# Token columns of the feed-forward products: 448 and 448 taken as 512 and 384, with one more float32 product

## The chip, the cores and the metric

The kernel runs on one core of a Trainium2 chip. The metric is device microseconds of one execution. The core has TensorE for matrix products (its results go to PSUM, which has eight banks of 512 float32 columns for each of 128 partitions), ScalarE and VectorE for elementwise work, GpSimd for elementwise work on SBUF, and SyncE, which issues the transfers. In the rows below they are PE (PEld for its weight loads), ACT, DVE, POOL and SP.

## The reference

Causal attention over 2 batches, 12 heads, 448 tokens and 64 columns a head, then two feed-forward blocks on the 896 tokens of both batches:

```python
attn = softmax(mask(q @ k.T / 8)) @ v       # per head; then as x: 896 x 768
a, b = x @ w1, x @ w2                       # 768 x 1024 each
x = ((a * b) @ w3) @ w_out                  # 1024 x 1024, 1024 x 768
h = x @ w_in                                # 768 x 2048
out = (maximum(h, 0) ** 2) @ w_out2         # 2048 x 768
```

All inputs are float32. The two weights w3 and w_out of the first block are multiplied with each other by the kernel, so that (a * b) meets one matrix W = w3 w_out of 1024 x 768.

## The kernel before

A float32 product is made of three products of the type float32r (L448): each operand is split into a high part and a rest, and high x high, high x rest and rest x high are added up in one PSUM bank. Plain float32 products are used where one product of full width stands alone (the attention, and `pause`).

The first part (L363 to L439) has attention, in an order written out by hand for TensorE, VectorE and ScalarE. In between it splits weights and multiplies w3 by w_out in slices of 384 columns (`w_half`, the tiles w of L69 with hl_wout). Attention leaves `xT`: the tokens as columns, both batches side by side, 2 x 448 = 896, in a high part and a rest.

What follows (L442 on) is the part that the change touches. Weights stand still on TensorE in tiles of 128 x 128 and tokens stream past them as columns, in two pieces of 448, one for each batch and each in a PSUM bank of its own. `products` (L446) gives the three float32r products of one weight tile for both pieces; the pieces take turns within each. The stages, in the names of the rows:

- **w** (`w12`, L475): 8 column tiles m of w1 and of w2, each summed over KD = 6 weight tiles. For the first EARLY = 2 tiles m, batch 0 is computed by itself ahead and batch 1 later; for the other six both pieces together. `ab` (L486) multiplies the two results (ScalarE copy, VectorE product) and splits them into `abT` (ScalarE, GpSimd).
- **h** (L510): 6 column tiles of W, each summed over KF = 8 tiles; `h_parts` splits into `hT` with ScalarE and VectorE. The last two tiles run together.
- **g** (L523) and **o** (L538), twice, for the two halves of 2048: g is 8 column tiles of w_in over 6 weight tiles, then relu and square on ScalarE (L533, L534) and the split into `gT` (ScalarE L119, GpSimd L120). o multiplies by the second w_out; here tokens stand still, 7 tiles of 128, and the 768 columns of w_out stream in two pieces of HN = 384.

`banks` (L455) gives out PSUM tiles in turn from two pools that hold the eight banks. `pause` (L462) is a plain float32 product of 64 columns of a weight tile with itself, into the bank that the next product overwrites, so that its result is of no use. It stands ahead of the first w product (after the 384-wide products of W) and ahead of the second g stage (after the 384-wide products of o).

The order in this part is that of a scheduler, which here keeps the order in which the code is written for TensorE. In the trace all products have line L69 (the helper `mm`), so tiles tell them apart: w, h, g, o. Split weights come through a ring of 8 buffers; loading, decoding and splitting them runs on SP, ScalarE and VectorE beside the products.

Of the kernel before, what the change touches and what calls it, by code (L numbers as in the profile page):

```python
# [8 lines left out]
F32 = mybir.dt.float32  # L9
F32R = mybir.dt.float32r  # L10
U32 = mybir.dt.uint32
AF = mybir.ActivationFunctionType
ALU = mybir.AluOpType
# [4 lines left out]
def attention_moe_moe2(ctx: ExitStack, tc: tile.TileContext, qk, v, w1, w2, w3, w_out, w_in2, w_out2, out):  # L18
# [13 lines left out]
    nc = tc.nc  # L32
    NP_ALL, P, S2 = qk.shape
    S = S2 // 2
    _, CP, _ = v.shape
    NT, DM = out.shape
    D = P // 2
    NCH = S // CP
    B = NT // S
    NPAIR = NP_ALL // B  # L40
    KD = DM // P
    KF = w1.shape[0]
    KF2 = w_in2.shape[0]
    HN = DM // 2
# [14 lines left out]
    EARLY = 2  # L59
# [8 lines left out]
    def mm(o, l, r, start, stop):  # L68
        return nc.tensor.matmul(o, l, r, start=start, stop=stop)  # L69
# [48 lines left out]
    def two_parts(hi, lo, x, engine=None):  # L118
        nc.scalar.copy(hi, x)  # L119
        (engine or nc.vector).tensor_tensor(lo, x, hi.bitcast(F32), op=ALU.subtract)  # L120
# [49 lines left out]
    def used(key):  # L170

        n = in_ring[key] + RING
        if n < len(ring):
            make(ring[n])
# [4 lines left out]
    with (  # L179
# [144 lines left out]
        parts = [key for key in order if not (key[0] == "w3" and key[1] < PLAIN)]  # L324
# [117 lines left out]
    tmp = ctx.enter_context(tc.tile_pool(name="tmp", bufs=4, reuse_waits="tile"))  # L442
    big2 = ctx.enter_context(tc.tile_pool(name="big2", bufs=1, reuse_waits="tile"))
    ps = ctx.enter_context(tc.tile_pool(name="ps", bufs=6, space=PSUM, reuse_waits="tile"))

    def products(o, wt, col, x, kk, start, stop, bs=(0, 1)):  # L446

        for s, t in ((0, 0), (0, 1), (1, 0)):  # L448
            for b in bs:
                mm(o[b], wt[:, s, col], x(kk)[:, t, b * S:(b + 1) * S],  # L450
                   start and (s, t) == (0, 0), stop and (s, t) == (1, 0))

    turn = [0]

    def banks(names, width=S):  # L455

        n = turn[0]
        turn[0] += len(names)
        where = [(ps_w, "w") if (n + i) % 8 < 2 else (ps, "mm") for i in range(len(names))]
        return [pool.tile([P, width], F32, tag=tag, name=m) for m, (pool, tag) in zip(names, where)]  # L460

    def pause(o, wt):  # L462

        x = wt[:, 0, :P].bitcast(F32)
        mm(o[:, :PAUSE], x, x[:, :PAUSE], True, True)

    def two_banks(name):
        return banks([f"{name}_{b}" for b in range(2)])

    def g_tiles(name):  # L470
        return [big2.tile([P, 2, NT], F32R, tag=f"G{m}", name=f"{name}{m}") for m in range(KF)]

    g_t = g_tiles("abT")

    def w12(m, bs):  # L475
        o = {}
        for nm in ("w1", "w2"):
            o[nm] = dict(zip(bs, banks([f"{nm}_{m}_{b}" for b in bs])))
            if nm == "w1" and m == 0 and 0 in bs:
                pause(o[nm][0], hls[nm, m])  # L480
            for kk in range(KD):
                products(o[nm], hls[nm, m], slice(kk * P, (kk + 1) * P), lambda c: xT[:, :, c], kk,
                         kk == 0, kk == KD - 1, bs)
        return o

    def ab(m, bs, o):  # L486
        for b in bs:
            a = tmp.tile([P, S], F32, tag="t", name=f"a{m}_{b}")
            nc.scalar.copy(a, o["w1"][b])
            nc.vector.tensor_tensor(a, o["w2"][b], a, op=ALU.mult)  # L490
            two_parts(*(g_t[m][:, s, b * S:(b + 1) * S] for s in range(2)), a, nc.gpsimd)

    os = [w12(m, (0,)) for m in range(EARLY)]
    for m in range(KF):
        if m < EARLY:
            ab(m, (0,), os[m])
        bs = (1,) if m < EARLY else (0, 1)
        ab(m, bs, w12(m, bs))
        used(("w1", m))
        used(("w2", m))  # L500

    hT = big.tile([P, 2, KD, NT], F32R, tag="X", name="hT")

    def h_parts(j, o):
        for b in range(2):
            hi, lo = (hT[:, s, j, b * S:(b + 1) * S] for s in range(2))
            nc.scalar.copy(hi, o[b])
            nc.vector.tensor_tensor(lo, o[b], hi.bitcast(F32), op=ALU.subtract)

    for js in [(j,) for j in range(KD - 2)] + [(KD - 2, KD - 1)]:  # L510
        o = [two_banks(f"h{j}") for j in js]
        for i in range(KF):
            for j, oj in zip(js, o):
                products(oj, hls["W", i], slice(j * P, (j + 1) * P), lambda c: g_t[c], i, i == 0, i == KF - 1)
            if len(js) > 1:
                used(("W", i))
        for j, oj in zip(js, o):
            h_parts(j, oj)

    acc = big.tile([P, NTT, DM], F32, tag="W", name="acc")  # L520
    for g in range(KF2 // KF):
        g_t = g_tiles(f"gT{g}_")
        for mi in range(KF):  # L523
            m = g * KF + mi
            o = two_banks(f"g{m}")
            if mi == 0 and g > 0:
                pause(o[0], hls["win2", m])
            for kk in range(KD):
                products(o, hls["win2", m], slice(kk * P, (kk + 1) * P), lambda c: hT[:, :, c], kk,
                         kk == 0, kk == KD - 1)  # L530
            for b in range(2):
                r = tmp.tile([P, S], F32, tag="t", name=f"r{m}_{b}")
                nc.scalar.activation(r, o[b], AF.Relu)  # L533
                nc.scalar.activation(r, r, AF.Square)  # L534
                two_parts(*(g_t[mi][:, s, b * S:(b + 1) * S] for s in range(2)), r, nc.gpsimd)
            used(("win2", m))
        ends = [(NTT - 2, NTT - 1)] if g == 0 else [(NTT - 2,), (NTT - 1,)]
        for ts in [(t,) for t in range(NTT - 2)] + ends:  # L538
            os = [banks([f"o{g}_{t}_{n}" for n in range(2)], HN) for t in ts]
            final = g > 0 and ts[0] == NTT - 1  # L540
            for ns in ((0,), (1,)) if final else ((0, 1),):
                for fi in range(KF):
                    w = hls["wout2", g * KF + fi]
                    for t, o in zip(ts, os):
                        for s, r in ((0, 0), (0, 1), (1, 0)):
                            for n in ns:
                                mm(o[n], g_t[fi][:, s, t * P:(t + 1) * P], w[:, r, n * HN:(n + 1) * HN],
                                   fi == 0 and (s, r) == (0, 0), fi == KF - 1 and (s, r) == (1, 0))
                    if len(ts) > 1:
                        used(("wout2", g * KF + fi))  # L550
            for t, o in zip(ts, os):
                for n in range(2):
                    a = acc[:, t, n * HN:(n + 1) * HN]
                    if g == 0:
                        if n == 0:
                            nc.scalar.copy(a, o[n])
                        else:
                            nc.vector.tensor_copy(a, o[n])
                    else:
                        nc.vector.tensor_tensor(a, o[n], a, op=ALU.add)  # L560
                        if final:
                            nc.sync.dma_start(out=out[t * P:(t + 1) * P, n * HN:(n + 1) * HN], in_=a)
                if g > 0 and not final:
                    nc.sync.dma_start(out=out[t * P:(t + 1) * P, :], in_=acc[:, t, :])
# [48 lines left out]
```

## Time and profile before

| | us |
|---|---|
| median of 3 runs | 577.47 (577.46 to 577.71) |
| the profiled execution | 577.6 |
| its span, first to last instruction | 575.4 |
| TensorE busy (products) | 563.9, 98% of the span |
| TensorE weight loads | 506.5, 88% |
| VectorE | 281.3, 49% |
| ScalarE | 268.2, 47% |
| GpSimd | 159.1, 28% |

The span is cut into attention (to about 161 us), w (to 280), h (to 339), g (to 397), o (to 455), g again (to 514) and o again (to 572). A busy TensorE is not a TensorE at its best, since a product's record covers its way through the array and overlaps the next one's. What tells the cost of a product in an unbroken stream is the length of the stream divided by its count, and that is how the rows are used below. The record's own length matters only where records of one kind are compared.

### The profile page before, as it was taken

What the parts mean: (1) busy time and instruction counts of PE and PEld (TensorE: products, weight loads), DVE (VectorE), ACT (ScalarE), POOL (GpSimd) and SP (SyncE); (2) the same over time, 40 slices, a digit from 0 to 9 for tenths busy, and PEclk for the clock granted to TensorE, in tenths of its full rate; (3) what the DMA queues carried; (4) which work ended last, traced back from release to release, by engine and by line L of the source; (5) the groups of instructions that cost most, each with busy time, mean ns of one, the idle gap of its engine ahead of it and who ended that gap; (6) DMA issues with size and microseconds to landing.
All of it is one profiled execution on the core that took longest, in us unless ns stands there. A gap on an engine that the chain in (4) does not pass through costs nothing.

```text
span 575.4 us, 8129 instructions
## 1 busy us (share of the span) xinstructions
PE 563.9 (98%) x3144; PEld 506.5 (88%) x3144; DVE 281.3 (49%) x567; ACT 268.2 (47%) x574; POOL 159.1 (28%) x140
## 2 busy tenths in 40 slices
PE   7899999999999999999999999999999999999997
PEld 5557777778989999999999999999999999999997
DVE  5987887767687544222210484555102854421011
ACT  5778777757865533222210456666002666640000
POOL 3367677776200312111100003333000023330000
PEclk9999999999999999999999999999999999999999
DMA  8854554233266633000000274333100763000111
GB/s 318 288 194 140 177 159 159 84 124 120 88 225 245 204 120 107 9 1 1 1 1 0 67 271 156 109 111 110 56 1 4 270 219 110 1 1 29 56 55 56
DMA packets 14823, 63.96 MB, mean 111 GB/s; under 512 B 1665, under 2 KB 1921, under 8 KB 14785
## 3 DMA queue, kind: packets, MB, share of 16 engines
q1 hardware_dynamic: 14784, 63.45, 32.2%
q8 instruction: 25, 0.41, 0.3%
q14 instruction: 14, 0.11, 0.1%
HBM read 60.69 MB, written 2.75 MB: 110 GB/s over the span
## 4 chain that ended last, share of the span: by engine, by line
PE 86%; DVE 6%; ACT 5%; issue 1%; DMA 1%; DVEq 0%; ACTq 0%
PE w L69 28%; PE g L69 20%; PE o L69 20%; PE h L69 10%; PE s L69 3%; PE x L69 2%; PE pp L273 2%; ACT p L245 2%; ACT pt L277 2%; DVE p L238 1%; DVE xw L108 1%; DMA qk<-in_qk 1%; ACT hl_wout L90 1%; DVE raw_wout L103 0%; DVE x_wout L108 0%
## 5 line engine op out<-in xcount | busy, mean ns | idle before, releaser
L69 PE MATMUL g<-hT,hl_win 128*128 128x448 f32 x576 | 117.2, 365 | 0.0
L69 PE MATMUL w<-xT,hl_w 128*128 128x448 f32 x576 | 117.0, 365 | 0.0
L69 PE MATMUL o<-hl_wout,gT 128*128 128x384 f32 x672 | 116.9, 334 | 0.0
L69 PEld LDWEIGHTS o<-hl_wout,gT 128*128 128x128 f32 x672 | 116.6, 188 | 0.1
L69 PEld LDWEIGHTS g<-hT,hl_win 128*128 128x128 f32 x576 | 108.1, 188 | 8.5
L69 PEld LDWEIGHTS w<-xT,hl_w 128*128 128x128 f32 x576 | 108.1, 188 | 8.5
L255 POOL TENSOR_SCALAR p<-p,st 112x448 f32<-112x448 f32 (+1 forms) x84 | 96.5, 1166 | 51.9 <-DVE st L252 23.3
L120 POOL TENSOR_TENSOR gT<-r,gT 128x448 fp32r<-128x448 f32 x32 | 39.1, 1245 | 195.8 <-ACT gT L119 128.7
L69 PE MATMUL w<-hl_wout,w 128*128 128x384 f32 x336 | 64.4, 342 | 0.5 <-DVE w L106 0.3
L245 ACT ACTIVATE p<-p,st 112x448 f32<-112x448 f32 (+1 forms) x96 | 49.7, 530 | 27.1 <-DVE st L238 27.0
L69 PEld LDWEIGHTS w<-hl_wout,w 128*128 128x128 f32 x336 | 57.4, 188 | 3.9 <-issue 0.9
L69 PE MATMUL h<-abT,hl_W 128*128 128x448 f32 x288 | 58.5, 365 | 0.0
L69 PEld LDWEIGHTS h<-abT,hl_W 128*128 128x128 f32 x288 | 54.1, 188 | 4.3
L120 POOL TENSOR_TENSOR abT<-a,abT 128x448 fp32r<-128x448 f32 x16 | 21.8, 1377 | 111.8 <-ACT abT L119 111.8
L238 DVE CUSTOM_DVE_ANT_0 p<-s,mask 112x448 f32<-112x448 f32 (+1 forms) x96 | 36.5, 441 | 7.0 <-PE s L69 7.0
L106 DVE TENSOR_TENSOR hl_wout<-x_wout,hl_wout 128x768 fp32r<-128x768 f32 x20 | 19.1, 957 | 37.9 <-ACT hl_wout L90 37.9
L533 ACT ACTIVATE r<-g 128x448 f32<-128x448 f32 x32 | 15.8, 542 | 40.8 <-PE g L69 40.8
L69 PE MATMUL s<-qk 64*112 64x448 f32 (+3 forms) x192 | 28.6, 443 | 4.1 <-DMA qk<-in_qk 4.1
L560 DVE TENSOR_TENSOR acc<-o,acc 128x384 f32<-128x384 f32 x14 | 7.2, 553 | 49.0 <-PE o L69 49.0
L273 PE MATMUL pp<-ident,p 112*112 112x112 f32 x240 | 27.9, 262 | 3.3 <-DVE st L238 1.6
L102 ACT ACTIVATE x_w<-raw_w 128x768 f32<-128x768 f32 (+1 forms) x30 | 24.4, 815 | 13.7 <-DVE hl_w L106 10.9
L273 PEld LDWEIGHTS pp<-ident,p 112*112 112x112 f32 x240 | 23.5, 134 | 8.0 <-issue 2.8
(62 smaller groups left out, 538.0 us busy)
## 6 DMA issues: line engine op xcount, KB each, us to landing
raw_wout<-in_w_out SPq DMA_DIRECT2D x24, 768.0 KB, 4.5
raw_w<-in_w SPq DMA_DIRECT2D x16, 768.0 KB, 4.3
raw_win<-in_w_in SPq DMA_DIRECT2D x16, 768.0 KB, 4.2
raw_w<-in_w SPq DMA_DIRECT2D x16, 512.0 KB, 3.9
qk<-in_qk SPq DMA_DIRECT2D x12, 448.0 KB, 5.1
v<-in_v SPq DMA_DIRECT2D x12, 224.0 KB, 2.6
out<-acc SPq DMA_DIRECT2D x6, 384.0 KB, 2.3
out<-acc SPq DMA_DIRECT2D x2, 192.0 KB, 1.8
```

The lines of the kernel that those rows point to most:

```text
L69: return nc.tensor.matmul(o, l, r, start=start, stop=stop)
L90: nc.scalar.copy(t[:, 0], x)
L102: nc.scalar.activation(y, high.bitcast(F32), AF.Prelu, scale=2.0 ** -112, alpha=-2.0 ** 32)
L106: nc.vector.tensor_tensor(t[:, 1], x, t[:, 0].bitcast(F32), op=ALU.subtract)
L120: (engine or nc.vector).tensor_tensor(lo, x, hi.bitcast(F32), op=ALU.subtract)
L238: nc.vector.tensor_tensor_reduce(e, ps[j, i], mask[:, S - (i + 1) * CP:], QS, 3.0e38, ALU.add, ALU.min, st_t[p][:, 0, j, i:i + 1],)
L245: nc.scalar.activation(e, e, AF.Exp, bias=st_t[p][:, 0, j, i:i + 1], scale=-1.0, accum_out=st_t[p][:, 1, j, i:i + 1])
L255: engine.tensor_scalar(e, e, st[:, 3, i:i + 1], None, ALU.mult)
L273: nc.tensor.transpose(x[:CP, o:o + CP], pt[:, off[i] + c * CP:off[i] + (c + 1) * CP], ident[:CP, :CP],)
L277: nc.scalar.copy(t[:, coff[g[0]]:coff[g[0]] + o], x[:CP, :o])
L533: nc.scalar.activation(r, o[b], AF.Relu)
L560: nc.vector.tensor_tensor(a, o[n], a, op=ALU.add)
```

## The change

For all products with both batches (six of the eight tiles m in w, all of h, all of g) the 896 columns are cut at 512 instead of at 448: pieces of 512 and 384. The first two tiles m of w, which are computed by batch, keep pieces of 448. PSUM tiles are always 512 columns wide, of which a piece uses what it needs. Everything that reads a bank (copy, product, relu, square, split) works on the same pieces. And `pause` comes a third time, ahead of the first product of tile m = 2 of w1, where the width goes from 448 to 512 and 384.

```diff
@@ -443,72 +443,75 @@
     big2 = ctx.enter_context(tc.tile_pool(name="big2", bufs=1, reuse_waits="tile"))
     ps = ctx.enter_context(tc.tile_pool(name="ps", bufs=6, space=PSUM, reuse_waits="tile"))
 
-    def products(o, wt, col, x, kk, start, stop, bs=(0, 1)):
+
+    BANK = 512
+    PARTS = (slice(0, BANK), slice(BANK, NT))
+    BATCHES = tuple(slice(b * S, (b + 1) * S) for b in range(B))
+
+    def products(o, wt, col, x, kk, start, stop, parts=PARTS):
 
         for s, t in ((0, 0), (0, 1), (1, 0)):
-            for b in bs:
-                mm(o[b], wt[:, s, col], x(kk)[:, t, b * S:(b + 1) * S],
-                   start and (s, t) == (0, 0), stop and (s, t) == (1, 0))
+            for d, b in zip(o, parts):
+                mm(d, wt[:, s, col], x(kk)[:, t, b], start and (s, t) == (0, 0), stop and (s, t) == (1, 0))
 
     turn = [0]
 
-    def banks(names, width=S):
+    def banks(names, widths):
 
         n = turn[0]
         turn[0] += len(names)
         where = [(ps_w, "w") if (n + i) % 8 < 2 else (ps, "mm") for i in range(len(names))]
-        return [pool.tile([P, width], F32, tag=tag, name=m) for m, (pool, tag) in zip(names, where)]
+        return [pool.tile([P, BANK], F32, tag=tag, name=m)[:, :w]
+                for m, w, (pool, tag) in zip(names, widths, where)]
 
     def pause(o, wt):
 
         x = wt[:, 0, :P].bitcast(F32)
         mm(o[:, :PAUSE], x, x[:, :PAUSE], True, True)
 
-    def two_banks(name):
-        return banks([f"{name}_{b}" for b in range(2)])
+    def part_banks(name, parts=PARTS):
+        return banks([f"{name}_{b.start}" for b in parts], [b.stop - b.start for b in parts])
 
     def g_tiles(name):
         return [big2.tile([P, 2, NT], F32R, tag=f"G{m}", name=f"{name}{m}") for m in range(KF)]
 
     g_t = g_tiles("abT")
 
-    def w12(m, bs):
+    def w12(m, parts):
         o = {}
         for nm in ("w1", "w2"):
-            o[nm] = dict(zip(bs, banks([f"{nm}_{m}_{b}" for b in bs])))
-            if nm == "w1" and m == 0 and 0 in bs:
+            o[nm] = part_banks(f"{nm}_{m}", parts)
+            if nm == "w1" and (m == 0 and parts == BATCHES[:1] or m == EARLY):
                 pause(o[nm][0], hls[nm, m])
             for kk in range(KD):
                 products(o[nm], hls[nm, m], slice(kk * P, (kk + 1) * P), lambda c: xT[:, :, c], kk,
-                         kk == 0, kk == KD - 1, bs)
+                         kk == 0, kk == KD - 1, parts)
         return o
 
-    def ab(m, bs, o):
-        for b in bs:
-            a = tmp.tile([P, S], F32, tag="t", name=f"a{m}_{b}")
-            nc.scalar.copy(a, o["w1"][b])
-            nc.vector.tensor_tensor(a, o["w2"][b], a, op=ALU.mult)
-            two_parts(*(g_t[m][:, s, b * S:(b + 1) * S] for s in range(2)), a, nc.gpsimd)
-
-    os = [w12(m, (0,)) for m in range(EARLY)]
+    def ab(m, parts, o):
+        for b, o1, o2 in zip(parts, o["w1"], o["w2"]):
+            a = tmp.tile([P, BANK], F32, tag="t", name=f"a{m}_{b.start}")[:, :b.stop - b.start]
+            nc.scalar.copy(a, o1)
+            nc.vector.tensor_tensor(a, o2, a, op=ALU.mult)
+            two_parts(g_t[m][:, 0, b], g_t[m][:, 1, b], a, nc.gpsimd)
+
+    os = [w12(m, BATCHES[:1]) for m in range(EARLY)]
     for m in range(KF):
         if m < EARLY:
-            ab(m, (0,), os[m])
-        bs = (1,) if m < EARLY else (0, 1)
-        ab(m, bs, w12(m, bs))
+            ab(m, BATCHES[:1], os[m])
+        parts = BATCHES[1:] if m < EARLY else PARTS
+        ab(m, parts, w12(m, parts))
         used(("w1", m))
         used(("w2", m))
 
     hT = big.tile([P, 2, KD, NT], F32R, tag="X", name="hT")
 
     def h_parts(j, o):
-        for b in range(2):
-            hi, lo = (hT[:, s, j, b * S:(b + 1) * S] for s in range(2))
-            nc.scalar.copy(hi, o[b])
-            nc.vector.tensor_tensor(lo, o[b], hi.bitcast(F32), op=ALU.subtract)
+        for b, ob in zip(PARTS, o):
+            two_parts(hT[:, 0, j, b], hT[:, 1, j, b], ob)
 
     for js in [(j,) for j in range(KD - 2)] + [(KD - 2, KD - 1)]:
-        o = [two_banks(f"h{j}") for j in js]
+        o = [part_banks(f"h{j}") for j in js]
         for i in range(KF):
             for j, oj in zip(js, o):
                 products(oj, hls["W", i], slice(j * P, (j + 1) * P), lambda c: g_t[c], i, i == 0, i == KF - 1)
@@ -522,21 +525,21 @@
         g_t = g_tiles(f"gT{g}_")
         for mi in range(KF):
             m = g * KF + mi
-            o = two_banks(f"g{m}")
+            o = part_banks(f"g{m}")
             if mi == 0 and g > 0:
                 pause(o[0], hls["win2", m])
             for kk in range(KD):
                 products(o, hls["win2", m], slice(kk * P, (kk + 1) * P), lambda c: hT[:, :, c], kk,
                          kk == 0, kk == KD - 1)
-            for b in range(2):
-                r = tmp.tile([P, S], F32, tag="t", name=f"r{m}_{b}")
-                nc.scalar.activation(r, o[b], AF.Relu)
+            for b, ob in zip(PARTS, o):
+                r = tmp.tile([P, BANK], F32, tag="t", name=f"r{m}_{b.start}")[:, :b.stop - b.start]
+                nc.scalar.activation(r, ob, AF.Relu)
                 nc.scalar.activation(r, r, AF.Square)
-                two_parts(*(g_t[mi][:, s, b * S:(b + 1) * S] for s in range(2)), r, nc.gpsimd)
+                two_parts(g_t[mi][:, 0, b], g_t[mi][:, 1, b], r, nc.gpsimd)
             used(("win2", m))
         ends = [(NTT - 2, NTT - 1)] if g == 0 else [(NTT - 2,), (NTT - 1,)]
         for ts in [(t,) for t in range(NTT - 2)] + ends:
-            os = [banks([f"o{g}_{t}_{n}" for n in range(2)], HN) for t in ts]
+            os = [banks([f"o{g}_{t}_{n}" for n in range(2)], [HN] * 2) for t in ts]
             final = g > 0 and ts[0] == NTT - 1
             for ns in ((0,), (1,)) if final else ((0, 1),):
                 for fi in range(KF):
```

The order of TensorE's instructions at this third pause, where w goes from one batch at a time to both (names are tile m and piece: `w1_2_0` is w1, m = 2, first piece; `hl_w1_2` its split weights). Before:

```order
L69 MATMUL w1_0_1_2072<-xT_67,hl_w1_0_1809 128x448 x18
L69 MATMUL w2_0_1_2091<-xT_67,hl_w2_0_1866 128x448 x18
L69 MATMUL w1_1_1_2138<-xT_67,hl_w1_1_1900 128x448 x18
L69 MATMUL w2_1_1_2157<-xT_67,hl_w2_1_1930 128x448 x18
L69 MATMUL w1_2_0_2199<-xT_67,hl_w1_2_1939 128x448
L69 MATMUL w1_2_1_2200<-xT_67,hl_w1_2_1939 128x448
```

and now:

```order
L69 MATMUL w1_0_448_2072<-xT_67,hl_w1_0_1809 128x448 x18
L69 MATMUL w2_0_448_2091<-xT_67,hl_w2_0_1866 128x448 x18
L69 MATMUL w1_1_448_2138<-xT_67,hl_w1_1_1900 128x448 x18
L69 MATMUL w2_1_448_2157<-xT_67,hl_w2_1_1930 128x448 x18
L69 MATMUL w1_2_0_2199<-hl_w1_2_1939 128x64
L69 MATMUL w1_2_0_2199<-xT_67,hl_w1_2_1939 128x512
L69 MATMUL w1_2_512_2200<-xT_67,hl_w1_2_1939 128x384
```

One instruction of 64 columns has come in; the products behind it have other widths and the same places.

On TensorE again, where the first o stage ends and the second g stage begins (`o0_6` is the last token tile of the first half, `g8` the ninth column tile of w_in). Before:

```order
L69 MATMUL o0_6_0_3899<-hl_wout2_7_3634,gT0_7_3180 128x384
L69 MATMUL o0_6_1_3900<-hl_wout2_7_3634,gT0_7_3180 128x384
L69 MATMUL g8_0_4081<-hl_win2_8_3919 128x64
L69 MATMUL g8_0_4081<-hT_2775,hl_win2_8_3919 128x448
L69 MATMUL g8_1_4082<-hT_2775,hl_win2_8_3919 128x448
```

and now:

```order
L69 MATMUL o0_6_0_3900<-hl_wout2_7_3635,gT0_7_3181 128x384
L69 MATMUL o0_6_1_3901<-hl_wout2_7_3635,gT0_7_3181 128x384
L69 MATMUL g8_0_4082<-hl_win2_8_3920 128x64
L69 MATMUL g8_0_4082<-hT_2776,hl_win2_8_3920 128x512
L69 MATMUL g8_512_4083<-hT_2776,hl_win2_8_3920 128x384
```

Nothing has moved here; the pause stands in the same place, and the pieces behind it are 512 and 384 columns wide.

## Rows read from the trace of the kernel before

**Rows 1.** Chain of waits, 155 us to the end: start, length, engine, tile, count

```profile
158.90 2.04 PE x L69 x16
160.94 119.26 PE w L69 x590
280.20 58.36 PE h L69 x288
338.57 58.37 PE g L69 x288
396.94 58.27 PE o L69 x336
455.20 58.60 PE g L69 x290
513.80 58.28 PE o L69 x336
572.08 0.02 issue
572.11 0.56 DVE acc L560
```

**Rows 2.** Page's groups: count | busy us, mean ns of one | idle us before

```profile
L69 PE MATMUL g<-hT,hl_win 128*128 128x448 f32 x576 | 117.2, 365 | 0.0
L69 PE MATMUL w<-xT,hl_w 128*128 128x448 f32 x576 | 117.0, 365 | 0.0
L69 PE MATMUL o<-hl_wout,gT 128*128 128x384 f32 x672 | 116.9, 334 | 0.0
...
L69 PE MATMUL h<-abT,hl_W 128*128 128x448 f32 x288 | 58.5, 365 | 0.0
```

**Rows 3.** Groups of ScalarE and GpSimd behind a g tile, 163 to 576 us

```profile
L534 ACT ACTIVATE r<-r 128x448 f32<-128x448 f32 x32 | 17.0, 584 | 0.0
L119 ACT CAST gT<-r 128x448 fp32r<-128x448 f32 x32 | 16.6, 569 | 0.0
L533 ACT ACTIVATE r<-g 128x448 f32<-128x448 f32 x32 | 15.8, 542 | 40.8 <-PE g L69 40.8
...
L120 POOL TENSOR_TENSOR gT<-r,gT 128x448 fp32r<-128x448 f32 x32 | 39.1, 1245 | 195.8 <-ACT gT L119 128.7 <-issue 67.2
```

**Rows 4.** TensorE in stretches of w, h, g, o: busy (count), clock, DMA share, GB/s

```profile
200.00:250.00 50.00, 50.00 (x248) 1.00 0.22 77
290.00:330.00 40.00, 40.00 (x199) 1.00 0.06 20
345.00:395.00 50.00, 50.00 (x249) 1.00 0.36 125
400.00:450.00 50.00, 50.00 (x290) 1.00 0.12 41
```

**Rows 5.** Settled products of w (one batch), h, o: record ns min/median/max, starts

```profile
L69 PE MATMUL w<-xT,hl_w x61: 362/365/369, 164.7 to 176.9; 128*128 128x448 f32 x61
...
L69 PE MATMUL h<-abT,hl_W x199: 362/365/369, 289.8 to 329.9; 128*128 128x448 f32 x199
...
L69 PE MATMUL o<-hl_wout,gT x290: 334/334/334, 399.8 to 449.8; 128*128 128x384 f32 x145
```

**Rows 6.** The same for the first seven products of o, behind g

```profile
L69 PE MATMUL o<-hl_wout,gT x7: 334/338/346, 396.8 to 397.8; 128*128 128x384 f32 x7
```

**Rows 7.** Timeline at two starts of a stage: last pieces of hT, gT, and their readers

```profile
344.11 0.62 DVE L508 TENSOR_TENSOR hT<-h,hT 128x448 fp32r<-128x448 f32 x1
...
338.40 6.85 PE L69 MATMUL g<-hT,hl_win 128*128 128x448 f32 x33
...
400.07 2.58 POOL L120 TENSOR_TENSOR gT<-r,gT 128x448 fp32r<-128x448 f32 x2 [4.71 <-issue]
...
396.78 8.51 PE L69 MATMUL o<-hl_wout,gT 128*128 128x384 f32 x48
```

## The prediction

> **What bounds the kernel now.** I read the chain of waits first, because it says which stage an edit must shorten. From 160.94 us on it holds TensorE alone: one unbroken run of products through every matrix of the two feed-forward blocks up to 572.08 us, and only a last VectorE add behind it [rows 1]. The edit touches w (w1 and w2), h (w3 w_out) and g (w_in), which stand in that run, and not the o products (the second w_out), which are 384 columns wide before and after. The groups of instructions say the same from the other side: g, w, o and h have 0.0 us idle ahead of them [rows 2]. So every nanosecond of a product's spacing counts here, and nothing that another engine does counts unless it becomes late. ScalarE, VectorE and GpSimd are followers with room: one g tile needs 542 + 584 + 569 ns of ScalarE for each half and 1245 ns of GpSimd [rows 3], so 3.4 and 2.5 us for both, against 36 products x 203 ns = 7.3 us of TensorE.
>
> Next I want the spacing of products by width. The chain's rows give it: h 58.36 us / 288 = 202.6 ns and g 58.37 / 288 = 202.7 ns for 448 columns, o 58.27 / 336 = 173.4 ns for 384 [rows 1]. The granted clock is 1.00 throughout [rows 4], that is the level of 2.4 GHz. I split a spacing into one cycle for a column and a rest; that split is mine. 448 columns are then 186.7 ns and the rest is 16.0 ns; 384 are 160.0 ns and the rest is 13.4 ns. The rest is thus neither nothing nor the same at both widths.
>
> The shape of the rest differs too. In a settled stretch of o all records of a product are alike, 334 at least and 334 at most; in settled stretches of h and w they run from 362 to 369 [rows 5]. A record covers more than the spacing (334 against 173), but what varies in it is when the next product could start. The w stretch belongs to the early products that use one batch alone, so the same tokens and no change of bank between two starts, and it has the same 362 to 369: the unevenness belongs to the width of 448, not to addresses or to taking turns between two halves.
>
> **The change, part by part.** What it replaces: pairs of 448 and 448 columns by pairs of 512 and 384. There are 6 x 2 x 6 x 3 = 216 such pairs in w (the first two column tiles stay at 448, since they are computed by batch), 8 x 6 x 3 = 144 in h and 16 x 6 x 3 = 288 in g, 648 in all. Columns and number of instructions stay the same, so the sum hangs on one number, the spacing of a 512-wide product, which the trace doesn't show, and on whether the 384-wide one keeps its 173.4 ns when a 512-wide one stands on either side. A pair now costs 58.37 / 144 = 405.4 ns.
>
> Bounds for 512. From below: one cycle a column, 213.3 ns, no rest at all. From above: the line through the two measured widths, 202.7 + (202.7 - 173.4) = 232.0 ns, or the longest excess that a 384-wide record shows while o is getting settled, 346 over 334 = 12 ns [rows 6], on top, so 244 ns. Between them stand three readings. (a) The rest of 13.4 ns goes with an even stream, and 512 is four times 128 as 384 is three times, while 448 is neither: 213.3 + 13.4 = 226.7, pair 400.1. (b) 512 gets the rest of 448, 16.0: 229.3, pair 402.7. (c) The rest grows with the width, by the line or in proportion (512 / 384 x 173.4 = 231.2): pair 404.6 to 405.4. I take (a): the row that 512 is nearest to in kind is the even one of 384, and the uneven row stands at the one width that is no multiple of 128. It is a choice between two points, not a proof.
>
> The sum at (a): 648 x (405.4 - 400.1) = 648 x 5.3 ns = 3.4 us less. At (b) 648 x 2.7 = 1.7 us less, at (c) 0 to 0.5 us less.
>
> The Trainium skill bears on this (TensorE: Matmul & The Clock Gate, section "Back-to-back issue gap"): an isolated warm product takes its columns / 2.4 GHz and some 2.5 ns. By that a pair would take 378.3 ns at 512 and 384 as at 448 and 448, and the pairs would be worth nothing. The trace doesn't bear out the amount (202.7 ns where the rule gives 189.2), yet its form, the same cost for each product whatever its width, is the second case below.
>
> What it adds: one pause, a plain float32 product of 64 columns that recurs as two records, ahead of the first 512-wide product of w1. Its price stands in the trace, since the second g stage has one and the first has none: 58.60 us with 290 records against 58.37 with 288 [rows 1], 0.23 us more. All of it is on the path. The pauses ahead of w and of the second g stage stand before and after. What the pause may keep away (a worse rhythm of the products behind it) no row prices; I count nothing for it.
>
> What it moves: the order shows no engine with another sequence, only widths, and some waits of TensorE on other products. Followers have pieces of 512 and 384 columns, together the same 896. Two places have little room. The last VectorE part of hT ends at 344.11 + 0.62 = 344.73, and the 34th g product, which reads it, starts at 338.40 + 33 x 0.2027 = 345.09: 0.36 us to spare [rows 7]. The last piece becomes 384 wide, 0.09 us less by its columns, while the 512-wide piece ahead of it is 0.09 us more; the room stays. The last gT part of GpSimd ends at 400.07 + 2.58 = 402.65 and is read from the 43rd o product, at 396.78 + 42 x 0.1734 = 404.06, with 1.4 us to spare [rows 7]; token tiles 0 to 3 now lie in the first piece entirely, so the second is wanted later still. Both nothing; if the first cover were gone it would cost some tenths of a microsecond once.
>
> Sum: the profiled execution took 577.6 us, of which 575.4 are its span; 577.6 - 3.4 + 0.2 = 574.4. The median of the runs is 0.1 lower, so **574.3 us**.
>
> **The rivals.** First, **the width doesn't matter**: readings (c), or a rest that belongs to the pair. For it speaks that 202.7 / 448 and 173.4 / 384 are 0.4524 and 0.4516 ns a column, nearly one number; against it, that a mere price per column wouldn't make one width even and the other uneven. The change then leaves all as it was but for 0 to 0.5 us less and the pause: 577.5 - 0.5 + 0.2 = 577.2, up to 577.7. That includes the case in which the edit doesn't do what it says.
>
> Second, **every change of width costs**: at the one place where the width changes without a pause, from g to o, the first seven products of 384 columns have records of 334 to 346 ns, median 338, before all settle at 334 [rows 6]. In o this is over after a handful, as all that follow are alike. In the new stream the width changes at every product, so it might never settle. The price: if each product is late by the median of 4 ns, over (a) to (c) the pair is 408.1 to 413.4, 1.8 to 5.2 us more in all, so 579.5 to 582.9 with the pause; at half the largest excess, 6 ns, up to 585.5. It decides from the point at which the loss per product exceeds half of what (a) gives, 2.6 ns. Against it speaks only that a settled rhythm can have a period of two, as that of 448 already has one longer than one.
>
> Third, **the follower becomes late** at the start of g, by the 0.36 us of room: it takes at most a few tenths off the gain and lies within the ranges of the others.
>
> **How the numbers follow.** I give the forecast 0.42, no matter of width 0.36, and a cost at each change 0.22. The forecast's own range runs from 573.2 (a rest somewhat under 13.4, some 1.7 ns a pair) to 576.0 (reading b). The whole range is 573.2 to 580.0: it takes in the first two cases and the lower end of the third, and leaves out the rest of the third and a rest far below 13.4 ns. Some 0.2% (1.2 us) is what a measurement of this kernel can tell from no change: faster by more than that 0.45, which is the forecast and a little of the second case; within it 0.33; slower 0.22.
>
> **What would show it.** In the changed kernel the chain's h row over 144 pairs: 57.6 us for (a), 58.0 for (b), 58.3 for (c), 58.8 or more where each change costs. The records of 512 and of 384 columns in a settled stretch of h: one number each for an even stream, a spread of some ns for an uneven one. The o stages stay at 58.27 us. The first w stage has two records of 64 columns more. The prediction is wrong if the o rows move too, if TensorE waits at the start of g or o, or if 384-wide products in h no longer follow each other at what the o row shows.

## The result and the profile after

The changed kernel takes **581.96 us** (median of 6 runs, 581.74 to 582.19), the kernel before 577.62 beside it: a ratio of **1.0076, 95% interval 1.0063 to 1.0089**. It is slower by 4.3 us, where 3.2 us faster was forecast, and lies above the stated range of 573.2 to 580.0. The profiled execution took 581.9 us with a span of 579.7.

The chain of waits of the changed kernel, in the same columns as [rows 1] (start, length, engine, tile, count):

```profile
160.85 121.19 PE w L69 x592
282.04 59.52 PE h L69 x288
341.56 59.49 PE g L69 x288
401.05 58.25 PE o L69 x336
459.30 58.79 PE g L69 x290
518.09 58.29 PE o L69 x336
```

Against [rows 1]: w is 1.93 us longer, h 1.16, the first g 1.12, the second g 0.19; both o stages are the same to 0.02 us. That is 4.40 us, and attention ends 0.09 us earlier: the 4.3 us by which the span is longer. TensorE waits for nothing in between, as before, so nothing became late: the products themselves have become slower. A pair of pieces takes 59.52 / 144 = 413.3 ns in h, where it took 405.3, and (58.79 - 0.23) / 144 = 406.7 ns in the second g stage. w has 216 such pairs, 216 x 8.0 = 1.7 us and 0.2 for the pause.

The records of settled stretches in h (290 to 330 us), the second g (470 to 510) and o (410 to 455): shortest/median/longest in ns, then the starts. They answer to [rows 5].

```profile
L69 PE MATMUL h<-abT,hl_W x195: 338/398/398, 289.7 to 329.8; 128*128 128x512 f32 x98, 128*128 128x384 f32 x97
...
L69 PE MATMUL g<-hT,hl_win x198: 337/366/395, 469.8 to 509.8; 128*128 128x384 f32 x99, 128*128 128x512 f32 x99
...
L69 PE MATMUL o<-hl_wout,gT x262: 334/334/334, 409.7 to 455.0; 128*128 128x384 f32 x131
```

In h a product is one of two lengths, 338 ns (384 columns) and 398 (512). So it is not an unsettled stream: it has settled, on a slow rhythm. A 384-wide record here is 4 ns longer than in o. From start to start, the trace's products in these stretches are (ns, 512- and 384-wide in turns):

```
h, 300 us:  237 176 237 176 238 176 237 176    pair 413.3
g, 480 us:  233 175 231 175 232 175 231 175    pair 406.7
```

One stream, two rhythms. The followers did what the prediction said: behind a g tile the three ScalarE operations take 1083, 1169 and 1138 ns for pieces of 512 and 384 together, as for two of 448 [rows 3]; GpSimd takes 2.6 us against 2.5, and nobody waits for them.

### The profile page after: what moved, and what is told of

Read it like the earlier page. It is cut to its first block, busy times and chain, and to the rows that moved or that the text cites. A ratio compares the mean times of both kernels' runs of the same rounds, so it can differ in the third digit from the quotient of the medians.

```text
span 579.7 us, 8132 instructions
## 1 busy us (share of the span) xinstructions
PE 568.1 (98%) x3146; PEld 499.0 (86%) x3146; DVE 282.3 (49%) x567; ACT 268.7 (46%) x574; POOL 161.2 (28%) x140
## 2 busy tenths in 40 slices
DMA packets 14822, 63.96 MB, mean 110 GB/s; under 512 B 1664, under 2 KB 1920, under 8 KB 14784
## 4 chain that ended last, share of the span: by engine, by line
PE 89%; DVE 5%; ACT 4%; issue 1%; DMA 1%; DVEq 0%
PE w L69 30%; PE g L69 20%; PE o L69 20%; PE h L69 10%; PE s L69 3%; PE x L69 3%; PE pp L273 3%; ACT p L245 1%; ACT pt L277 1%; DVE p L238 1%; DVE xw L108 1%; DMA qk<-in_qk 1%; DVE raw_wout L103 0%; DVE x_wout L108 0%; ACT hl_wout L90 0%
## 5 line engine op out<-in xcount | busy, mean ns | idle before, releaser
L69 PE MATMUL w<-xT,hl_w 128*128 128x512 f32 (+1 forms) x576 | 118.9, 368 | 0.0
L69 PE MATMUL g<-hT,hl_win 128*128 128x512 f32 (+1 forms) x576 | 118.5, 367 | 0.0
L69 PEld LDWEIGHTS w<-xT,hl_w 128*128 128x128 f32 x576 | 105.5, 188 | 12.8
L69 PEld LDWEIGHTS g<-hT,hl_win 128*128 128x128 f32 x576 | 104.6, 188 | 13.4
L120 POOL TENSOR_TENSOR gT<-r,gT 128x512 fp32r<-128x512 f32 (+1 forms) x32 | 41.1, 1307 | 196.3 <-ACT gT L119 130.1
L69 PE MATMUL h<-abT,hl_W 128*128 128x512 f32 (+1 forms) x288 | 59.7, 368 | 0.0
L69 PEld LDWEIGHTS h<-abT,hl_W 128*128 128x128 f32 x288 | 52.4, 188 | 7.1
L120 POOL TENSOR_TENSOR abT<-a,abT 128x512 fp32r<-128x512 f32 (+2 forms) x16 | 21.9, 1384 | 113.7 <-ACT abT L119 113.7
L536 ACT ACTIVATE r<-g 128x512 f32<-128x512 f32 (+1 forms) x32 | 15.8, 542 | 43.1 <-PE g L69 43.1
L69 PE MATMUL s<-qk 64*112 64x112 f32 (+3 forms) x192 | 28.5, 435 | 4.2 <-DMA qk<-in_qk 4.2
```

Of the source, the lines that this page charges most:

```text
L536: nc.scalar.activation(r, ob, AF.Relu)
```

## The experiments

Each ratio is against the kernel before, run on the same chip. The settled pair is the length of the chain's h row over 144, unless another stage is named.

### 1. One width at a time, in blocks of 18

```diff
-            for kk in range(KD):
-                products(o[nm], ..., parts)
+            for d, b in zip(o[nm], parts):
+                for kk in range(KD):
+                    products([d], ..., [b])
```

(and the same in g from its second tile on, and in the first four column tiles of h; the last two of h have runs of six)

> The changed kernel, with each piece of 512 and of 384 columns summed in one go: 18 products of 512, then 18 of 384 in w and g (24 and 24 in h), so that the width changes once in 18 products and not at each. The first g tile and the last two column tiles of h keep short turns (1 and 6), for their waits. If a change of width is what costs, a stretch of 512 columns settles at 226.7 to 232 ns and one of 384 at 173.3: the kernel comes out at 574 to 577.5 us, under the changed one's 582.0. If 512 columns by themselves cost the 237.3 ns that they have in the changed kernel, with 384 back at 173.3, the pair is 410.7 and the kernel some 580.5 us.

Measured: 577.1 us, ratio 0.9998 (0.9988 to 1.0007), 5 us better than the changed kernel with the same widths and the same number of products. The start-to-start times of one 384-wide block in w, behind a 512-wide one:

```
170 175 178 185 175 182 173 174 173 173 174 173 174 173 173 174 172 174
```

The first six are unsettled, as the first products of o are behind g [rows 6]; then it is 173.3 ns. The 512-wide block ahead of it ends on 226 to 228. So 512 columns by themselves are not dear: reading (a) of the prediction, 226.7 ns, is what a settled stream of 512 takes. What the blocks lose is the unsettled start of each.

### 2. Three of one width, then three of the other

```diff
-        for s, t in ((0, 0), (0, 1), (1, 0)):
-            for d, b in zip(o, parts):
+        for d, b in zip(o, parts):
+            for s, t in ((0, 0), (0, 1), (1, 0)):
```

> The changed kernel with the three products of a weight tile on one piece in a row: three of 512, then three of 384, so a third as many changes of width. If each change has a price, the loss against a pair at the settled rate is a third of the changed kernel's: from 413.3 ns per pair to about 403 to 408, and 575.5 to 579 us. If the price sits on 512 itself, nothing moves: 580.5 to 582 us.

Measured: 579.31 us, ratio 1.0034 (1.0020 to 1.0047); h 58.72 us, 407.8 ns a pair. The pair lies at the upper end of what was expected of a price for each change, the time 0.3 us above it: with a third of the changes 7.8 of the 13.3 ns are left, where a third was expected. It could still be read as such a price; experiment 7 shows that it must not be.

### 3 and 4. Without the third pause; with pauses ahead of h and the first g

```diff
-            if nm == "w1" and (m == 0 and parts == BATCHES[:1] or m == EARLY):
+            if nm == "w1" and m == 0 and parts == BATCHES[:1]:
```

> The changed kernel without the third pause. In the trace of the changed kernel pairs take 413.3 ns in w, h and the first g stage, and 406.7 ns in the second g stage, so the stream seems to have two rhythms, and what stands ahead picks one. If the pause ahead of the third w tile picks the slow one, w, h and the first g come out at 406.7 or below without it: 648 - 144 pairs x -6.6 ns less the pause, 579 us or less. If the rhythm is slow whatever precedes it, 581.8 us, only the pause's 0.2 us less. If the pause protects, slower than 582.

Measured: 581.35 us, ratio 1.0072 (1.0055 to 1.0088). w has 120.98 us against 121.19, the pause's 0.2; h stays at 59.52, the first g at 59.49. The third pause neither causes the slow rhythm nor keeps it away.

```diff
+        if js[0] == 0:
+            pause(o[0][0], hls["W", 0])
...
-            if mi == 0 and g > 0:
+            if mi == 0:
```

> The changed kernel with two pauses more, ahead of h and of the first g stage. If a pause sets the rhythm of what follows, h or the first g (or both) leave 413.3 ns per pair, by 6.7 ns x 144 pairs = 1 us each if they go to 406.7, minus 0.2 us for each pause: 580.4 to 581.5 us. If the rhythm belongs to the stage and not to the entry, both stay at 413.3 and the kernel is at 582.4 us.

Measured: 580.92 us, ratio 1.0064 (1.0049 to 1.0079). h goes from 59.52 to 58.79 us with two records more, so to 406.7 ns a pair: the entry does pick the rhythm. In the first g the stream runs at 406.7 for some 5 us and then falls back to 413.3. It does so at 346 to 350 us, where pieces of one width stand next to each other for a moment, as they also do at 347 to 351 us of the changed kernel: the scheduler seems to mix the products of the first two g tiles there, so it keeps the written order on TensorE less strictly than said in the part on the kernel before.

### 5 and 6. Long runs of one width

Every second matrix begins with the piece with which the last one ended, so that 36 products of one width follow on each other (5), or two tiles at a time, 72 to 144 (6). h does its 512-wide sums for four column tiles, then the 384-wide ones. The third pause and that ahead of the second g stage are gone.

```diff
+            for n in ((1, 0), (0, 1))[mi % 2]:
+                b = PARTS[n]
...
+                for kk in range(KD):
+                    products([d], hls["win2", m], ..., [b])
```

> Runs of one width made longer: each weight matrix of w and g sums its two pieces in one go, and every second one begins with the piece with which the last one ended (512, 384, 384, 512, ...), 36 products of one width in a row; h does all its 512-wide sums of four column tiles, then the 384-wide ones. 33 changes of width in place of 1296; no third pause, and none ahead of the second g stage, which begins with 384 columns as o ended. If a change costs a handful of unsettled products (some 38 ns in all on the 512 side and 26 ns on the 384 side, from the blocks of 18) and a settled pair is 400.0 ns: 577.5 - 648 x 5.3 - 0.2 + 33 x 0.032 = 574.9 us, faster than both kernels. If the blocks of 18 gained from something else than fewer changes, no more than their 577.1 us.

Measured: 575.91 us, ratio 0.9974 (0.9963 to 0.9984). It is 1.0 us short of the expected 574.9, and most of that is a wait, the only one of TensorE behind attention (who waited for what: us, times, longest):

```profile
PE o L69 <- DVE hl_wout L106: 0.7, 1, 0.7
```

A part of w_out comes late in the first o stage: on VectorE its split stands behind the decoding of a part of w_in, which has waited 4.4 us for its transfer. That the transfers come later because this order gives ring buffers back later is likely, but not shown. w took 118.53 us and the second g 57.87.

> The same with two matrix pairs (w) or two column tiles (g) at a time: runs of 72 to 144 products of one width, 16 changes. If the price sits on the change: 17 changes fewer than with runs of 36, another 0.5 us less, 574.4 us. If weights come late, since a ring buffer is released only after two tiles, TensorE shows waits and the gain is eaten. If changes don't matter: 577 us.

Measured: **574.46 us, ratio 0.9948 (0.9936 to 0.9961)**, as expected. Of the 2.9 us gained, 0.2 are the pause ahead of the second g stage. The chain's h and first g rows and, below, the records of h in a run of 512 and in one of 384:

```profile
279.10 57.71 PE h L69 x288
336.81 57.76 PE g L69 x288
```

```profile
L69 PE MATMUL h<-abT,hl_W x64: 389/389/389, 284.7 to 298.9; 128*128 128x512 f32 x64
...
L69 PE MATMUL h<-abT,hl_W x100: 334/334/334, 304.8 to 321.9; 128*128 128x384 f32 x100
```

57.71 / 144 = 400.8 ns for 512 and 384 together, with three changes in the whole stage. Both widths are as even as [rows 5] show o.

### 7. Other widths in turns: 480 and 416

```diff
-    PARTS = (slice(0, BANK), slice(BANK, NT))
+    PARTS = (slice(0, 480), slice(480, NT))
```

> The changed kernel with the cut at 480 instead of 512, so pieces of 480 and 416 columns, a width change at each product as before, neither width as regular as 384. If any change of width costs, whatever the widths: pairs over 405.3 ns, up to 413, 578 to 582 us. If the loss belongs to 512 next to 384 alone, the pair is at 405.3 or less and the kernel at 577.7 us.

Measured: **574.12 us, ratio 0.9941 (0.9926 to 0.9957)**. The first branch of the expectation failed: the width changes at every product, and the kernel is faster than the one before. The second had the pair right (405.3 ns or less), but its 577.7 us went with 405.3 itself; a gain was not foreseen. The chain's h and g rows and the records of h:

```profile
278.99 57.60 PE h L69 x288
336.59 57.65 PE g L69 x288
```

```profile
L69 PE MATMUL h<-abT,hl_W x201: 351/351/373, 289.8 to 329.8; 128*128 128x416 f32 x101
```

In this stretch the trace has 210 and 190 ns from start to start, in turns without an exception, 400.0 ns a pair. That every change of width has a price, whatever the widths, is thereby refuted, although experiments 1, 2, 5 and 6 all fitted it.

### 8. Control: the blocks with 448 and 448

```diff
-    PARTS = (slice(0, BANK), slice(BANK, NT))
+    PARTS = (slice(0, 448), slice(448, NT))
```

(on experiment 1, without the third pause)

> Control: the order of the blocks of 18, with pieces of 448 and 448 and without the third pause, so that only the order differs from the kernel before. If order alone does nothing, 577.5 us and 202.67 ns for a product, and what the blocks of 512 and 384 show is due to widths. If order alone gains or costs (a wait at the start of h or g), it shows here as that many microseconds.

Measured: 577.56 us, ratio 1.0015 (0.9999 to 1.0031), w at 119.26, h and g at 58.37 us, as in [rows 1] to 0.01. The order of the blocks shows no effect of its own.

### 9 to 11. 464 and 432; 496 and 400; 480 and 416 without the third pause

The edits are those of experiments 7 and 3 with other numbers.

> The changed kernel with the cut at 464: pieces of 464 and 432 columns in turns. Measured so far: pairs of 400.0 ns for 480 and 416, 405.3 for 448 and 448, 413.3 or 406.7 for 512 and 384, so a change of width by itself isn't what costs. If nearness to equal widths is what helps, this pair is at 400 to 405 ns and the kernel at 574 to 577.7 us. If each pair has a rhythm of its own with no such order, anything from 400 to 413 ns, 574 to 582 us.

> The same with 496 and 400 columns, between the pair that gained (480, 416) and the one that lost (512, 384). If the loss grows with the difference of the widths: between 400 and 413 ns a pair, 575 to 580 us. If each pair has a rhythm of its own: no order, 574 to 582 us.

> 480 and 416 columns without the third pause. If this pair has one rhythm, whatever stands ahead of it, all stages stay at 400.0 ns and the kernel is 0.2 us faster than with the pause, 573.9 us. If the entry picks one, w (and h and g behind it) leave 400.0 ns, as 512 and 384 have 413.3 ns behind one entry and 406.7 behind another: 575 us or more.

Measured: 579.54 us for 464 and 432 (ratio 1.0037, 1.0023 to 1.0052; pair 408.3 ns), 578.48 for 496 and 400 (1.0020, 1.0011 to 1.0029; 406.7), 574.08 for 480 and 416 without the pause (**0.9945, 0.9930 to 0.9959**; 400.0). The difference of the widths puts them in no order: a pair whose widths differ by 32 columns takes 408.3 ns, by 64 it takes 400.0, by 96 406.7. Widths alone are not compared here, though, since each cut also moves the place where the second piece begins (13 to 18). And the good rhythm of 480 and 416 needs no entry.

### 12. Seven entries in one kernel

```diff
-    def pause(o, wt):
+    def pause(o, wt, n=PAUSE):
...
+        if js[0] < 3:
+            pause(o[0][0], hls["W", 0], (128, 96, 16)[js[0]])
```

(32 columns in w; 16, 48 and 112 in the second g)

> The changed kernel (512 and 384) with pauses of other lengths at seven places: 32 columns ahead of the third w tile, 128, 96 and 16 ahead of the first three column tiles of h, 16, 48 and 112 ahead of the first, third and fifth g tile of the second half. If the entry picks the rhythm, the stretches behind them differ, each at 413.3 or 406.7 ns for a pair, perhaps at a third value such as 400.0. If the two rhythms belong to the stages, w and h stay at 413.3 and the second g at 406.7. Each pause costs some 0.2 us.

Measured: 583.01 us in one run. Pairs of 512 and 384 run at 413.3 ns behind the pause of 32 columns in w, at 406.7 behind 128 and 96 in h, at 413.3 behind 16; in the second g at 413.3 behind 16 and at 406.7 from the one of 48 on. The streams ahead of 128 (h) and 48 (g) were slow and turned fast there, those ahead of 16 turned or stayed slow; 96 and 112 found the fast one and kept it. Two rhythms, no third, and the entry picks one. The length of the pause doesn't decide by itself: 64 columns led to the slow rhythm ahead of w and to the fast one ahead of h (4) and of the second g.

### 13 to 15. Where the pieces lie, and which comes first

With the cut, the second piece's place in memory moved too. Here it alone moves: read 32 tokens, 128 bytes a partition, earlier (13 with 512 and 384, 14 with 480 and 416); 15 cuts at 384, so that the narrow piece comes first.

```diff
-                mm(d, wt[:, s, col], x(kk)[:, t, b], ...)
+                c = slice(b.start - 32, b.stop - 32) if b.stop == NT and len(parts) > 1 else b
+                mm(d, wt[:, s, col], x(kk)[:, t, c], ...)
```

> The changed kernel (512 and 384), with the second piece read 32 tokens earlier in the joint products (tokens 480 to 863 in place of 512 to 895), so that the last 32 tokens are left out and others come twice: widths and order as before, addresses other. If the rhythm belongs to widths and entry alone: 413.3 ns a pair in w, h and the first g, 406.7 in the second g, 582.0 us. If it belongs to where the pieces lie: other values, 574 to 585 us.

> 480 and 416 columns, with the second piece read 32 tokens earlier (448 to 863 in place of 480 to 895; the last 32 tokens are left out). If widths alone make the 400.0 ns: unchanged, 574.1 us. If the place of the second piece makes them: over 400 ns a pair and 575 us or more.

> The changed kernel with the cut at 384, so that the 384-wide piece comes first and the 512-wide second. In turns the stream is the same but for its first product. If widths alone count, pairs at 413.3 or 406.7 ns, 579 to 582 us, the rhythm picked by the entry; the second g stage now starts with the width that o ended on. If which piece comes first counts, something else, 400 to 405 ns.

Measured, one run each: 577.12, 578.14 and 580.50 us. The h row of 13 and the records of its h:

```profile
280.11 58.24 PE h L69 x288
```

```profile
L69 PE MATMUL h<-abT,hl_W x200: 332/364/396, 289.7 to 329.9; 128*128 128x512 f32 x100
```

At unchanged widths, 512 and 384 went from 413.3 to 404.4 ns a pair, 480 and 416 from 400.0 to 406.7 (h 58.56 us; 403.3 in the second g). The widths alone don't make the rhythm; the place counts. In 15 the two known rhythms appear, 406.7 ns in w and h and 413.3 in most of g.

### 16 to 18. Equal widths; 256 bytes; the weights

> The kernel before in widths (448 and 448, no third pause), with the second piece read 32 tokens (128 bytes a partition) earlier, from 416: the last 32 tokens are left out, others come twice. If where a piece begins sets the rest of a product, the pair leaves 405.3 ns although both widths are unchanged: anything from 400 to 413 ns, 574 to 583 us. If equal widths settle whatever the place: 405.3 ns and 577.5 us.

> 480 and 416 columns, the second piece read 64 tokens (256 bytes) earlier, where 32 tokens earlier gave 403.3 to 406.7 ns. All pieces that settled evenly so far begin on multiples of 256 bytes (0, 1536, 1792, 2048). If only the place within 256 bytes counts, the pair is back at 400.0 ns and the kernel at 574.1 us; if the distance counts in another way (pieces that follow on each other, a longer period), another value.

```diff
+        if len(parts) > 1:
+            n = 32 if col.stop < DM else -32
+            col = slice(col.start + n, col.stop + n)
```

> The changed kernel (512 and 384), with the weights of the joint products read 32 columns (128 bytes) further on (earlier for the last tile), so that wrong columns are multiplied: the pieces lie as they did, only the weight tiles lie elsewhere. If the rest of a product comes from the moving columns meeting the weight load in SBUF, the place of one to the other counts and the pair leaves 413.3 and 406.7 ns. If it comes from the moving columns alone, both stay and the kernel is at 582.0 us.

Measured, one run each. 16 (448 and 448, the second piece 128 bytes earlier): 579.22 us, h 58.88, 408.9 ns a pair against 405.3. 17 (480 and 416, 256 bytes earlier): 574.12 us, h 57.60, 400.0 ns, the unshifted kernel's time. 18 (512 and 384, only the weights moved by 128 bytes): 580.84 us, h 59.04, 410.0 ns against 413.3; its second g went the other way, to (59.26 - 0.23) / 144 = 409.9 ns against 406.7. The h rows of 16, 17 and 18, and the second g of 18:

```profile
280.86 58.88 PE h L69 x288
```

```profile
278.95 57.60 PE h L69 x288
```

```profile
281.37 59.04 PE h L69 x288
...
457.66 59.26 PE g L69 x290
```

The records of h in experiments 14, 16, 17 and 18:

```profile
L69 PE MATMUL h<-abT,hl_W x198: 350/365/383, 289.8 to 329.9; 128*128 128x480 f32 x99, 128*128 128x416 f32 x99
```

```profile
L69 PE MATMUL h<-abT,hl_W x198: 365/366/368, 289.7 to 330.0; 128*128 128x448 f32 x198
```

```profile
L69 PE MATMUL h<-abT,hl_W x202: 351/362/373, 289.8 to 330.0; 128*128 128x416 f32 x101
```

```profile
L69 PE MATMUL h<-abT,hl_W x197: 334/392/400, 289.8 to 330.0; 128*128 128x512 f32 x99, 128*128 128x384 f32 x98
```

Moved by 128 bytes, the even stream of 480 and 416 has spread out (350 to 383, where unshifted there are only 351 and 373); moved by 256 bytes it is back on its two values (the median falls between them). And with the moving columns untouched, other places for the weights turn the two values of the slow rhythm (338 and 398) into a spread of 334 to 400. So what the rest of a product depends on includes where the moving columns lie and where the weight tiles lie.

No place is good for all widths. Counted from the start of its row, whose 896 x 4 bytes are a multiple of 256, the second piece begins at 0 within 256 bytes for the cuts at 448 and 512, and at 64, 128 and 192 for 464, 480 and 496. At 0 the pair of 448 and 448 takes 405.3 ns, at 128 it takes 408.9 in h; 512 and 384 take 413.3 or 406.7 at 0 and 404.4 at 128; 480 and 416 take 400.0 at 128 and 403.3 to 406.7 at 0. The even stream of 480 and 416 in experiment 7 thus begins at 1920 bytes, no multiple of 256, which the expectation of 17 overlooks.

## Why the prediction was wrong

- **What bounds the kernel** was right: one stream of products to the end, before and after, and each nanosecond of it counted. The changed kernel's 4.3 us are all in products of the edited stages, and o stayed at 58.25 us.
- **The split into columns and a rest** held, and reading (a) too, as far as it goes: 512 columns settle at 226.7 ns, 13.3 over their columns, when only 512-wide products follow on each other. Experiment 6 has that in long runs, and gains 2.9 us.
- **The step that failed** is the one named in the prediction as the second thing on which the sum hangs: that a 384-wide product keeps its 173.4 ns, and a 512-wide one its 226.7, when they take turns. The sum was made with values of streams of one width, and no row of before has a settled stream of two. In turns the pair is 413.3 ns (237.3 + 176.0) or 406.7, not 400.1. 504 pairs of w, h and the first g at +8.0 and 144 of the second g at +1.3 against 405.3 make 4.2 us, and 0.2 are the pause: that is the loss. Against the forecast's 400.1 ns the same pairs make the 7.6 us by which it missed.
- **Addresses** were ruled out on too thin a ground. The rows of w with one batch alone [rows 5] showed 362 to 369 ns as the alternating ones did, and I read that as "not addresses". But the two starts they compare, 0 and 1792 bytes, are the same within 256 bytes; experiments 14 and 16 show that a move by 128 bytes counts, and 17, for one cut, that one by 256 doesn't. In 16 the records of the same 448 columns run from 365 to 368: the unevenness doesn't belong to the width alone. A comparison in which the suspected cause doesn't vary rules nothing out.
- **Even is not cheap.** Reading (a) was chosen because the row of 384 was the even one. In turns evenness says nothing of the price: the changed kernel's h is even (338 and 398) and slow, while experiment 13 is spread out (332 to 396) and 8.9 ns a pair faster at the same widths.
- **The second rival**, every change of width costs, gave 579.5 to 582.9 us and so the right time, for 0.22, and its sign (h at 58.8 us or more) came. That was luck: its mechanism was wrong, since 480 and 416 change width as often and run at 400.0 ns, and the new stream did settle, in h with a period of two. That such a rhythm can exist was put against the rival; it came, and it was the slow one. The sign that 384-wide products in h no longer follow each other as in o (176.0 ns against 173.4) did point at the step that failed.
- **The pause** cost what it was said to: w is 0.21 us shorter without it. It was counted as keeping nothing away, and experiment 3 agrees, for this place.
- **Followers** were right: no wait at the start of g or o.
- **The chances**: 0.22 for slower was low for a sum that rested on one number with no row. Pair lengths found in all: 400.0 to 413.3 ns, on both sides of the 405.3 of before. A forecast of no change with both sides open would have said what the rows knew.

What stays open is how the chip makes these rests. Shown is on what they depend: widths, places within 256 bytes of the columns and of the weights, and for 512 and 384 the entry. That column reads and weight loads get into each other's way in SBUF fits all of it, but no run shows it directly, and none tells it from reads that are slower at some places by themselves. The recorded length of a weight load in h tells nothing for either: its median is 187 or 188 ns in the kernel before, the changed one and experiments 13, 14 and 16 to 18, and the longest is 192, in 14 and 18.

The Trainium skill (TensorE: Matmul & The Clock Gate, section "Step-by-step: what each phase is for") says that TensorE has two independent read ports into SBUF, so that loading the next weights takes no read bandwidth from the running product. Experiment 18 shows that the place of the weights matters to these float32r products even so: moving only the weights by 128 bytes changed a pair in h from 413.3 to 410.0 ns. Whether the running product loses by it or the next one only starts at another time, no run here shows.

## What to carry to other kernels

In an unbroken stream of products, measure the stream that will run: the settled time of a product among its own kind doesn't hold in turns with another width, and a change of cut moves addresses as well as widths. Where TensorE bounds a stage, try a few cuts of the moving columns: here 480 and 416 without the third pause took 0.55% less than 448 and 448, 512 and 384 with it 0.76% more, and long runs of one width, with one pause fewer, 0.52% less. And a suspect (an address, an entry) is cleared only by a comparison in which it changes.

## What the runs showed of the hardware

- The rest of a float32r product over one column a cycle at 2.4 GHz (the granted clock was 1.00) is 13.3 ns in settled streams of 384 or of 512 columns and 16.0 in one of 448; for a pair in turns, at the places of an unshifted cut, it is 26.7 (480 and 416), 33.3 or 40.0 ns (512 and 384).
- A stream can have two lasting rhythms at the same work: 512 and 384 ran at 413.3 ns a pair from w through h and the first g, some 200 us, and at 406.7 behind another entry. Ahead of h a pause of 64 or of 128 columns led to the fast one, one of 16 to the slow one.
- After a change to a run of one width some six products of 384 columns are unsettled (170 to 185 ns) before it stays at 173.3.
- Moving operands by 128 bytes a partition is worth up to 8.9 ns a pair (413.3 to 404.4); moving the second piece by 256 bytes left 480 and 416 at 400.0.
